# Attention into a mixture of experts: the product with V in plain float32 on 64 columns a head, a third buffer for raw weights, later places for attention's matmuls, last outputs in halves

## The chip, the core and the metric

The kernel runs on one core of a Trainium2 chip. TensorE (PE) does matmuls into PSUM, VectorE (DVE) and ScalarE (ACT) work on SBUF and PSUM, GpSimd (POOL) does two reductions over partitions, and SyncE (SP) issues nearly all transfers. The metric is the time of one execution in microseconds of device time, and lower is better.

## What is computed

Block-causal attention over 4 batches of 8 heads (576 positions, 64 numbers a head), whose output, with the heads side by side, is the input of 4 expert networks; each token mixes the experts by its own probabilities.

```
scores = scale * np.matmul(q, k.transpose(0, 1, 3, 2))
mask = block_i >= block_j              # blocks of 64 positions
scores = np.where(mask, scores, -1000000000.0)
attn = np.exp(scores - max); attn = attn / (sum + 1e-09)
x = np.matmul(attn, v)                 # -> [2304, 512]
...
for e in range(4):
    h = np.maximum(x @ w1[e], 0.0)     # 512 -> 1024
    out += p[:, e:e + 1] * (h @ w2[e]) # 1024 -> 512
```

(Condensed; all in float32.)

## The kernel before

**Tokens.** The 2304 tokens are worked on in five blocks: block 0 holds the first 64 positions of all batches (256 tokens), blocks 1 to 4 hold positions 64 to 575 of one batch each (512 tokens). For a block, the experts run as 32 chunks (4 experts by 8 slices of 128 hidden units). A chunk is 12 matmuls x·w1 into a bank `h` (`mm1`, line 1035) and, one chunk later, h·w2 into the accumulators `acc` (`mm2`, line 1080: 12 matmuls in blocks 1 to 4, 6 in block 0).

**Split numbers.** The experts' operands are split into a high and a low part, and three products (high·high, high·low, low·high) in a fast float32 form ("fp32r") stand for one float32 product. For the weights, ACT or DVE casts the raw tile to its high part (line 340), and DVE subtracts to get the low part (line 347: `w1l`, `w2l`). Raw tiles lie in `w1r` and `w2r`, two buffers each; a buffer is free again when its low part is done. After mm1, ACT makes `hh` (line 1052) and DVE `hl` (line 1054).

**Attention** runs beside the experts, one block ahead, in 16 units (4 head pairs of 4 batches). Units 0 to 3 run beside block 0 and are "plain"; units 4 to 15 run beside blocks 1 to 3 and are "split". In all of them keys lie on the partitions of the score tile `S`, queries along it: five pieces of 512, 448, 320, 192 and 64 columns, for two heads. A unit multiplies Q and K into PSUM banks `att` (lines 527; 539 and 540 in split units), copies each bank to `S` (ACT mostly) and takes the running maximum `cm` on DVE; POOL reduces the maximum over partitions (line 696); DVE subtracts it; ACT takes exponentials. There are two `att` banks, and a split unit fills seven banks' worth of scores, so a bank's next product waits until ACT and DVE have read the bank.

The product with V differs. In plain units, exponentials are taken piece by piece, plain float32 matmuls multiply them with V, head 0 into partitions 0 to 63 of a bank and head 1 into 64 to 127 (line 777, 64 columns of V each), and another four matmuls with ones sum the probabilities. In split units, each head's probabilities are split into `PH` and `PL` and V into `VS`; per head, four matmuls with PH, one with the last 64 keys in plain float32 and four with PL (line 809) make a bank whose upper and lower halves are added. The sums come from POOL (line 733), after the pieces have been added up in `S`.

**Order.** All engines' instruction lists come from one planner (`Flow`) that simulates engines with estimated costs and picks the next instruction. `late(op, by)` adds `by` ns to the distance that it wants from the instructions that an operation depends on, and half of it to the distance from the last use of the operation's buffers (`est`, line 107). Score products of split units have `LAG` = 1500, the products with V of split units half of it, plain units none. Engines run their lists strictly in order.

Of the kernel before, what the change touches and what calls it, by code (L numbers as in the profile page):

```python
# [15 lines left out]
MASK_BLOCK = 64  # L16
# [20 lines left out]
LAG = 1500.0  # L37
# [34 lines left out]
class Flow:  # L72
# [134 lines left out]
def kernel(  # L207
# [65 lines left out]
    bufs("w1r", 2, [P, KC, P])  # L273
    bufs("w2r", 2, [P, DM])
# [7 lines left out]
    bufs("vr", 1, [P, MAXT, 2, D])  # L282
# [5 lines left out]
    bufs("VS", 2, [P, MAXT, 4, D], F32R)  # L288
    bufs("VJ", 2, [P, 2, 3, D])
# [94 lines left out]
    def unit(u, ua, us, ju, pu, ph, job, dst, c):  # L384
# [5 lines left out]
        wide, narrow = [x for x in pcs if x[2] > NARROW and not plain], [x for x in pcs if x[2] <= NARROW or plain]  # L390
        ce = sum(x[2] for x in wide)
# [67 lines left out]
        def v_thread():  # L459
            yield ("until", lambda: now[0] >= gate[u])  # L460
            vals, jv, got = [], [], []
            n = len(wide)
            VS = None
            VJ = yield (fl.take("VN", u) if plain else fl.take("VJ", us))
            if n:
                vr = yield fl.take("vr", us)
                VS = yield fl.take("VS", us)
                for h in range(2):
                    vals.append((yield dma(vr.tile[:, :n, h, :], v[b, h0 + h, :P * n].rearrange("(t p) d -> p t d", p=P),
                                           n * P * 256, u=[vr], prio=pr + 0.005)))  # L470
            keep = sorted(j for j, *_ in narrow if j is not None)
            for h in range(2):
                if plain:
                    jv.append((yield dma(VJ.tile[:, VJ.tile.shape[1] - 1, 2 * h, :], v[b, h0 + h, q1 - P:q1], P * 256,
                                         u=[VJ], prio=pr + 0.005)))
                elif odd:
                    jv.append((yield dma(VJ.tile[64 * h:64 * h + 64, VJ.tile.shape[1] - 1, 1, :], v[b, h0 + h, q1 - MASK_BLOCK:q1], 64 * 256,
                                         u=[VJ], prio=pr + 0.005)))
                if keep:
                    jv.append((yield dma(VJ.tile[:, :len(keep), 2 * h, :],  # L480
                                         v[b, h0 + h, P * keep[0]:P * keep[-1] + P].rearrange("(t p) d -> p t d", p=P),
                                         len(keep) * P * 256, u=[VJ], prio=pr + 0.005)))
            if n:
                vs = VS.tile[:, :n]
                a = yield a_copy(vs[:, :, 0:4:3, :], vr.tile[:, :n], n * 128, vals, [vr, VS], pr + 0.005)
                l = yield tt(BOTH, vs[:, :, 1:3, :], vr.tile[:, :n], vs[:, :, 0:4:3, :], SUB, n * 128, [a], [vr, VS],
                             pr + 0.005)
                got += [a, l]
                fl.give(vr)
            st["v"] = (VS, VJ, got, jv)  # L490

# [18 lines left out]
        def s_thread():  # L510
# [31 lines left out]
            for h, ps_list in banks:  # L542
                if plain:
# [15 lines left out]
                    m = yield op("pe", 300.0 + (2 * sum(ws) + ws[0] - sum(abs(x - y) for x, y in zip(ws, ws[1:]))) / 1.2,  # L559
                                 fn, need(0), [*two, KK] + Q, pr)  # L560
# [94 lines left out]
        def by_piece(Sb, Sv, mx, mv, m):  # L655
# [8 lines left out]
            def sum_up():  # L664
# [3 lines left out]
                for i, (_, a, w, c0) in enumerate(todo[1:]):  # L668
# [18 lines left out]
        def m_thread():  # L687
# [13 lines left out]
            st["P"] = {}  # L701
            st["exp"] = []

            if plain:
                yield from by_piece(Sb, Sv, mx, mv, m)
                return
            subs = []
            for _, a, w, c0 in pcs:
                sv, mb = Sv[:, :, c0:c0 + w], mv[:, :, a - q0:W]
                subs.append((yield tt("dve", sv, sv, mb, SUB, 2 * w, [m] + st["evac"], [Sb, mx], pr)))  # L710
            fl.give(mx)

            def exp_head(h):
                PH = PL = a = l = None
                j = yield op("act", 0.833 * C + 95, lambda _: nc.scalar.activation(
                    Sv[:, h, :C], Sv[:, h, :C], AF.Exp, scale=scale), subs, [Sb], pr)
                if wide:
                    PH = yield fl.take("PH", pu + h)
                    PL = yield fl.take("PL", pu + h)
                    a = yield a_copy(PH.tile[:, :ce], Sv[:, h, :ce], ce, [j], [Sb, PH], pr)  # L720
                    l = yield tt("dve", PL.tile[:, :ce], Sv[:, h, :ce], PH.tile[:, :ce], SUB, ce, [j, a], [Sb, PH, PL], pr)
                st["P"][h] = (PH, PL, a, l, Sb, j)

            for h in range(2):
                yield from exp_head(h)

            got = [x for h in range(2) for x in st["P"][h][2:4] + st["P"][h][5:]]
            for _, a, w, c0 in pcs[1:]:
                acc = Sv[:, :, a - q0:W]
                got = [(yield tt("dve", acc, acc, Sv[:, :, c0:c0 + w], ADD, 2 * w, got, [Sb], pr))]  # L730
            st["sums"] = []
            for h in range(2):
                st["sums"].append((yield op("pool", 150 + 6.3 * W, lambda _, h=h: nc.gpsimd.partition_all_reduce(  # L733
                    Sv[:, h, W:2 * W], Sv[:, h, :W], P, RED.add), got, [Sb], pr)))
# [3 lines left out]
        fl.spawn(pv_flow(st, q0, dst, c, W, wide, narrow, C, plain, pr, bank_tag))  # L738
# [13 lines left out]

    def pv_flow(st, q0, dst, c, W, wide, narrow, C, plain, pr, bank_tag):
        yield ("until", lambda: "v" in st)
        VS, VJ, vv, jv = st["v"]
        xs = yield fl.take("xs")
        rc = yield fl.take("rc", st["ua"])
        parts, sums = [], []
        if plain:
            yield ("until", lambda: "sums" in st)  # L760
            sa, sv = st["sums"]
            PJ, pj = st["P"][1][4:]
            two = []
            for _ in range(2):
                two.append((yield fl.take("att", None, bank_tag)))

            def fn(_):

                for x, todo in zip(two, (narrow, [(None, None, W, 0)])):
                    for i, (j, _a, w, c0) in enumerate(todo):  # L770
                        for g in range(2):
                            if x is two[0]:
                                lhsT = VJ.tile[:, VJ.tile.shape[1] - 1 if j is None else j, 2 * g, :]
                                rhs = PJ.tile[:, g * C + c0:g * C + c0 + w]
                            else:
                                lhsT, rhs = VJ.tile[:, 0, 1, :], sa.tile[:, g * W:g * W + W]
                            nc.tensor.matmul(out=x.tile[64 * g:64 * g + 64, W - w:W], lhsT=lhsT, rhs=rhs,  # L777
                                             start=(i == 0), stop=(i == len(todo) - 1))

            m = yield op("pe", 450.0 + (C + W) / 0.6, fn, jv + pj + sv, [*two, VJ, PJ, sa], pr)  # L780
# [8 lines left out]
            sums.append((yield op([("act", 0.833 * W + 55), ("dve", 1.04 * W + 70)], 0, fn, [m], [two[1], rc], pr)))  # L789
            parts.append((yield a_copy(xs.tile[:, :W], two[0].tile[:, :W], W, [m], [two[0], xs], pr, True)))  # L790
            fl.give(*two)
        for h in range(0 if plain else 2):
            yield ("until", lambda: h in st.get("P", ()))
            PH, PL, a, l, PJ, pj = st["P"][h]
            pb = yield fl.take("att", None, bank_tag)
            ps = pb.tile
# [416 lines left out]
```

## Time and profile before

| | |
|---|---|
| median of 3 runs | 931.5 us (931.19 to 933.13) |
| the profiled execution | 932.45 us, of which its span is 930.7 us |
| granted TensorE clock, mean | 0.999 of full speed |
| HBM read / written | 102.40 MB / 4.72 MB |

The span runs from the first to the last instruction of the profile; the 1.75 us between it and the execution's time lie around it. Busy time of an engine is time with at least one instruction on it; a matmul's duration in the profile includes the pipeline's depth, so the pace of matmuls is read from one start to the next.

### The profile page before, as it was taken

How to read it: one execution, taken by the hardware profiler on the slowest of the kernel's cores; microseconds unless marked ns; L12 is line 12 of the kernel's file. 1: busy time of each engine (PE TensorE's matmuls, PEld its weight loads, DVE VectorE, ACT ScalarE, POOL GpSimd, SP SyncE). 2: the span in 40 equal slices, each digit the busy share in tenths (PEclk: the TensorE clock that was granted, in tenths of full speed). 3: DMA queues.
4: the chain of work that ended last, by engine and by line, in shares of the span. 5: the costliest groups of instructions: out<-in, count | busy, mean ns of one | idle time of the engine just before them, and what ended most of it. 6: DMA issues, size and time to landing. Idle time of an engine off the chain costs nothing.

```text
span 930.7 us, 12721 instructions
## 1 busy us (share of the span) xinstructions
PE 915.3 (98%) x4398; PEld 750.8 (81%) x4398; DVE 728.9 (78%) x1291; ACT 438.2 (47%) x774; POOL 138.7 (15%) x57
## 2 busy tenths in 40 slices
PE   8999999999999999999999999999999999999998
PEld 4677788888887888887888888888888888888886
DVE  7789999989897888878988888888988754445442
ACT  3577765655463454454454545464534322322220
POOL 1111101222103201212131202012121200000000
PEclk9999999999999999999999999999999999999999
DMA  9755466534532445351623545343423343333321
GB/s 166 181 163 165 136 154 189 116 115 93 145 85 80 113 140 137 108 135 46 149 72 100 128 121 154 104 105 113 116 90 90 92 148 102 92 100 94 100 57 45
DMA packets 236162, 107.97 MB, mean 116 GB/s; under 512 B 131393, under 2 KB 213313, under 8 KB 236097
## 3 DMA queue, kind: packets, MB, share of 16 engines
q1 hardware_dynamic: 232928, 106.38, 42.8%
q10 hardware_dynamic: 3168, 0.79, 0.5%
q8 instruction: 34, 0.56, 0.2%
q14 instruction: 32, 0.25, 0.1%
HBM read 102.40 MB, written 4.72 MB: 115 GB/s over the span
## 4 chain that ended last, share of the span: by engine, by line
PE 90%; DVE 4%; DMA 3%; ACT 1%; issue 1%; SPq 1%; DVEq 0%; ACTq 0%
PE acc L1080 40%; PE h L1035 40%; PE att L809 4%; PE att L539 2%; PE att L540 2%; DMA w1r<-in_moe_w_dram 1%; SPq L334 1%; PE acc L777 1%; PE att L777 1%; DVE w2l L347 1%; DMA S<-in_v_dram 1%; DVE cm L347 1%; PE att L527 1%; DVE w1l L347 0%; DMA w2r<-in_moe_w_dram 0%
## 5 line engine op out<-in xcount | busy, mean ns | idle before, releaser
L1035 PE MATMUL h<-xh,w1h 128*128 128x512 f32 (+1 forms) x640 | 237.9, 372 | 0.0
L1035 PE MATMUL h<-xh,w1l 128*128 128x512 f32 (+1 forms) x640 | 236.1, 369 | 1.6 <-DVE w1l L347 1.6
L1035 PE MATMUL h<-xl,w1h 128*128 128x512 f32 (+1 forms) x640 | 235.6, 368 | 0.1
L1080 PE MATMUL acc<-w2h,hh 128*128 128x512 f32 x576 | 227.0, 394 | 0.0
L1080 PE MATMUL acc<-w2h,hl 128*128 128x512 f32 x576 | 224.7, 390 | 1.0 <-DVE hl L1054 1.0
L1080 PE MATMUL acc<-w2l,hh 128*128 128x512 f32 x576 | 224.6, 390 | 0.0
L1052 ACT ACTIVATE hh<-h 128x512 fp32r<-128x512 f32 (+1 forms) x160 | 88.9, 556 | 184.6 <-PE h L1035 183.5
L347 DVE TENSOR_TENSOR w2l<-w2r,w2h 128x512 fp32r<-128x512 f32 x160 | 112.9, 706 | 56.2 <-ACT w2h L340 55.8
L340 ACT CAST w2h<-w2r 128x512 fp32r<-128x512 f32 x148 | 92.2, 623 | 136.1 <-PE acc L1080 132.0
L1035 PEld LDWEIGHTS h<-xh,w1l 128*128 128x128 f32 x640 | 120.4, 188 | 22.7 <-DVE w1l L347 2.4
L1035 PEld LDWEIGHTS h<-xh,w1h 128*128 128x128 f32 x640 | 120.5, 188 | 21.0 <-issue 1.2
L1035 PEld LDWEIGHTS h<-xl,w1h 128*128 128x128 f32 x640 | 120.6, 188 | 19.8 <-DVE xl L347 0.3
L1054 DVE SCALAR_TENSOR_TENSOR hl<-h,hh 128x512 fp32r<-128x512 f32 (+1 forms) x160 | 100.6, 629 | 35.9 <-ACT hh L1052 35.4
L1080 PEld LDWEIGHTS acc<-w2h,hl 128*128 128x128 f32 x576 | 108.1, 188 | 25.0 <-DVE hl L1054 1.9
L1080 PEld LDWEIGHTS acc<-w2h,hh 128*128 128x128 f32 x576 | 108.3, 188 | 23.9 <-issue 2.5
L347 DVE TENSOR_TENSOR w1l<-w1r,w1h 128x512 fp32r<-128x512 f32 x160 | 119.3, 745 | 8.2 <-ACT w1h L340 4.4
L1080 PEld LDWEIGHTS acc<-w2l,hh 128*128 128x128 f32 x576 | 108.3, 188 | 20.0
L733 POOL PARTITION_ALL_REDUCE S<-S x24 | 79.8, 3374 | 242.4 <-DVE S L347 223.9
L696 POOL PARTITION_ALL_REDUCE mx<-cm x16 | 54.4, 3398 | 355.8 <-DVE cm L347 270.3
L340 ACT COPY S<-att 128x512 f32<-128x512 f32 (+2 forms) x90 | 48.7, 542 | 71.3 <-DVE att L609 48.6
L340 ACT CAST w1h<-w1r 128x512 fp32r<-128x512 f32 x116 | 71.6, 619 | 19.4 <-DMA w1r<-in_moe_w_dram 19.1
L347 DVE TENSOR_TENSOR S<-S,mx 128x1024 f32<-128x1024 f32 (+4 forms) x80 | 60.0, 790 | 5.4 <-POOL mx L696 5.4
(135 smaller groups left out, 862.3 us busy)
## 6 DMA issues: line engine op xcount, KB each, us to landing
w1r<-in_moe_w_dram SPq DMA_DIRECT2D x160, 256.0 KB, 2.8
w2r<-in_moe_w_dram SPq DMA_DIRECT2D x160, 256.0 KB, 2.8
qr<-in_q_dram SPq DMA_DIRECT2D x112, 64.0 KB, 2.3
kr<-in_k_dram SPq DMA_DIRECT2D x64, 72.0 KB, 2.8
out_dram<-o SPq DMA_DIRECT2D x16, 256.0 KB, 2.3
vr<-in_v_dram SPq DMA_DIRECT2D x24, 128.0 KB, 2.6
VN<-in_v_dram SPq DMA_DIRECT2D x8, 128.0 KB, 3.1
S<-in_k_dram SPq DMA_DIRECT2D x4, 128.0 KB, 4.7
```

The lines of the kernel that those rows point to most:

```text
L340: o = op(engs, 0, lambda e: nc.scalar.copy(dst, src) if e == "act" else nc.vector.tensor_copy(dst, src), r, u, prio)
L347: o = op(engs, 0, lambda e: ENG[e].tensor_tensor(out=dst, in0=a, in1=b, op=alu), r, u, prio)
L539: nc.tensor.matmul(out=o, lhsT=KK.tile[:, at:at + n], rhs=Hv[:, hs, lo:W], start=True, stop=False)
L540: nc.tensor.matmul(out=o, lhsT=KK.tile[:, at:at + n], rhs=Lv[:, hs, lo:W], start=False, stop=True)
L696: lambda _: nc.gpsimd.partition_all_reduce(mx.tile[:, :2 * W], src, P, RED.max),
L733: st["sums"].append((yield op("pool", 150 + 6.3 * W, lambda _, h=h: nc.gpsimd.partition_all_reduce(Sv[:, h, W:2 * W], Sv[:, h, :W], P, RED ...
L777: nc.tensor.matmul(out=x.tile[64 * g:64 * g + 64, W - w:W], lhsT=lhsT, rhs=rhs, start=(i == 0), stop=(i == len(todo) - 1))
L809: nc.tensor.matmul(out=o, lhsT=lhsT, rhs=rhs, start=(i == 0), stop=(i == n - 1))
L1035: nc.tensor.matmul(out=ps[:, :n], lhsT=s.tile[:, ks], rhs=x.tile[:, kc, :n], start=(kc == 0 and m == 0), stop=(kc == KC - 1 and m == 2),)
L1052: a = yield op("act", 0.833 * n + 55, lambda _: nc.scalar.activation(hh.tile[:, :n], ps[:, :n], AF.Relu), [mm], [pb, hh], 0.0)
L1054: l = yield op("dve", 1.04 * n + 70, lambda _: nc.vector.scalar_tensor_tensor(out=hl.tile[:, :n], in0=ps[:, :n], scalar=0.0, in1=hh.tile[: ...
L1080: nc.tensor.matmul(out=acc, lhsT=s.tile[:, ts], rhs=w.tile, start=(f == 0 and m == 0), stop=(f == FC - 1 and m == 2))
```

## The change

- Split units now do the product with V as plain units do: float32 matmuls, 64 columns a head, both heads in one bank, probabilities straight from `S`. PH, PL, VS, VJ and the additions of halves are gone. The sums of split units stay with POOL, but are taken from `sa`, the tile in which plain units add up their pieces, into a new tile `sb`. Exponentials are taken piece by piece in all units.
- `w1r` and `w2r` get a third buffer.
- `LAG` becomes 2000, the planner wants the whole lag (not half) from a buffer's last use, and plain units' score products get half a LAG.
- In the last block, the last expert's multiply-and-add of each token tile and its transfer to memory are done in two halves of 256 columns, on the queues of SP and ACT.

```diff
-LAG = 1500.0
+LAG = 2000.0
...
-                if b.base + self.LAT + op.lag / 2 > t:
-                    t = b.base + self.LAT + op.lag / 2
+                if b.base + self.LAT + op.lag > t:
+                    t = b.base + self.LAT + op.lag
...
-    bufs("w1r", 2, [P, KC, P])
-    bufs("w2r", 2, [P, DM])
+    bufs("w1r", 3, [P, KC, P])
+    bufs("w2r", 3, [P, DM])
...
+    bufs("sb", 1, [P, 2 * MAXW])
...
+                sb = yield fl.take("sb", us)
+                sums = []
                 for h in range(2):
-                    st["P"][h] = (None, None, None, None, Sb, exps)
-                st["sums"] = (sa, got)
+                    sums.append((yield op("pool", 150 + 6.3 * W, lambda _, h=h: nc.gpsimd.partition_all_reduce(
+                        sb.tile[:, h * W:h * W + W], sa.tile[:, h * W:h * W + W], P, RED.add), got, [sa, sb], pr)))
+                fl.give(sa)
+                st["sums"] = (sb, sums)
...
-                    m = yield op("pe", 300.0 + (2 * sum(ws) + ws[0] - sum(abs(x - y) for x, y in zip(ws, ws[1:]))) / 1.2,
-                                 fn, need(0), [*two, KK] + Q, pr)
+                    m = yield late(op("pe", 300.0 + (2 * sum(ws) + ws[0] - sum(abs(x - y) for x, y in zip(ws, ws[1:]))) / 1.2,
+                                 fn, need(0), [*two, KK] + Q, pr), LAG / 2)
...
+            for x, todo in zip(two, (pcs, [(None, None, W, 0)])):
+                for i, (j, _a, w, c0) in enumerate(todo):
+                    for g in range(2):
+                        if x is two[0]:
+                            lhsT = VJ.tile[:, j, 2 * g, :] if j is not None else VJ.tile[:, nj, 2 * g if plain else 1, :]
+                            rhs = PJ.tile[:, g * C + c0:g * C + c0 + w]
+                        else:
+                            lhsT, rhs = VJ.tile[:, 0, 1, :], sa.tile[:, g * W:g * W + W]
+                        nc.tensor.matmul(out=x.tile[64 * g:64 * g + 64, W - w:W], lhsT=lhsT, rhs=rhs,
+                                         start=(i == 0), stop=(i == len(todo) - 1))
+
+        m = yield late(op("pe", 450.0 + (C + (W if plain else 0)) / 0.6, fn, jv + pj + sv,
+                          [*two, VJ, PJ] + ([sa] if plain else []), pr), 0.0 if plain else LAG / 2)
...
-            for x, split, dep in ((PH, True, a), (PJ, False, pj), (PL, True, l)):
...
-            x = yield a_copy(rc.tile[hi, :W], ps[lo, :W], W, [m], [pb, rc], pr, True)
-            parts.append((yield tt("dve", xs.tile[hi, :W], ps[hi, :W], rc.tile[hi, :W], ADD, W, [m, x], [pb, rc, xs], pr)))
...
+        if e == E - 1 and bi == len(BLOCKS) - 1:
+
+            (p0, tok, n), = segments(bi, t)
+            o = outs[bi, t]
+            for x, q_ in enumerate(("sp", "act")):
+                c = slice(DM // 2 * x, DM // 2 * (x + 1))
+                d = yield op("dve", 1.04 * DM / 2 + 130, lambda _, c=c: nc.vector.scalar_tensor_tensor(
+                    out=o.tile[:, c], in0=acc[:, c], scalar=pn, in1=o.tile[:, c], op0=MUL, op1=ADD), [mm], [o], 0.0)
+                yield dma(out[tok:tok + n, c], o.tile[p0:p0 + n, c], n * DM * 2, [d], [o], 6.0, q_)
+            return
```

On PE, at a split unit's product with V (unit 7), the order before is two groups a head with expert matmuls (lines 1035 and 1080) around them; this is head 0:

```order
L1035 MATMUL h_123<-xh_90,w1l_66 128x512
L809 MATMUL att_128<-PH_115,VS_104 128x512
L809 MATMUL att_128<-PH_115,VS_104 128x448
L809 MATMUL att_128<-PH_115,VS_104 128x320
L809 MATMUL att_128<-PH_115,VS_104 128x192
L809 MATMUL att_128<-S_112,VJ_106 128x64
...
L809 MATMUL att_128<-PL_113,VS_104 128x512
L809 MATMUL att_128<-PL_113,VS_104 128x448
L809 MATMUL att_128<-PL_113,VS_104 128x320
L809 MATMUL att_128<-PL_113,VS_104 128x192
L1080 MATMUL acc_126<-w2h_69,hh_81 128x512
```

On PE, a unit's whole product with V in the change is one run of ten matmuls, of which each row stands for both heads:

```order
L718 MATMUL att_123<-S_109,VN_105 64x512 x2
L718 MATMUL att_123<-S_109,VN_105 64x448 x2
L718 MATMUL att_123<-S_109,VN_105 64x320 x2
L718 MATMUL att_123<-S_109,VN_105 64x192 x2
L718 MATMUL att_123<-S_109,VN_105 64x64 x2
```

Eighteen matmuls a unit have become ten, each with 64 columns of V instead of 128.

On PE, at the score products of unit 7's second head before, the bank `att_129` is used for the pieces of 320 and 192, then 15 expert matmuls and the two of the other bank stand ahead of its next use, the piece of 448:

```order
L540 MATMUL att_129<-LL_102,KK_100 128x192
...
L1035 MATMUL h_123<-xh_90,w1l_66 128x512
L539 MATMUL att_128<-HH_101,KK_100 128x512
L540 MATMUL att_128<-LL_102,KK_100 128x512
...
L1035 MATMUL h_123<-xl_92,w1h_62 128x512
L1035 MATMUL h_123<-xh_90,w1l_66 128x512
L539 MATMUL att_129<-HH_101,KK_100 128x448
```

At the same place of the change (where the roles of the two banks are swapped) 21 expert matmuls stand between them:

```order
L507 MATMUL att_122<-LL_103,KK_101 128x192
...
L506 MATMUL att_123<-HH_102,KK_101 128x512
L507 MATMUL att_123<-LL_103,KK_101 128x512
...
L998 MATMUL acc_119<-w2h_70,hl_86 128x512
L506 MATMUL att_122<-HH_102,KK_101 128x448
```

So a bank's next product has moved back by six expert matmuls here.

On SP's queue, early in the program, before (`w1r_78` and `w2r_80` are chunk 1's weights, `w1r_77` and `w2r_79` chunk 2's, `kr_94` keys and `VN_108` values of the next unit):

```order
L334 DMA w1r_78<-in_moe_w_dram 128x4x128
L334 DMA w2r_80<-in_moe_w_dram 128x512
L334 DMA kr_94<-in_k_dram 32x18x32 x3
L334 DMA w1r_77<-in_moe_w_dram 128x4x128
L334 DMA kr_94<-in_k_dram 32x18x32
L334 DMA VN_108<-in_v_dram 128x64
L334 DMA w2r_79<-in_moe_w_dram 128x512
```

and in the change, where chunk 2 has buffers of its own (`w1r_79`, `w2r_82`) and `w1r_77` and `w2r_80` already hold chunk 3's:

```order
L324 DMA w1r_78<-in_moe_w_dram 128x4x128
L324 DMA w1r_79<-in_moe_w_dram 128x4x128
L324 DMA w2r_81<-in_moe_w_dram 128x512
L324 DMA w2r_82<-in_moe_w_dram 128x512
L324 DMA kr_96<-in_k_dram 32x18x32
L324 DMA w1r_77<-in_moe_w_dram 128x4x128
L324 DMA kr_96<-in_k_dram 32x18x32 x2
```

Chunk 2's weights have moved ahead of the next unit's keys, and chunk 3's among them.

## Rows read from the trace of the kernel before

**Rows 1.** The page: span, and each engine's busy time with instruction count.

```profile
span 930.7 us, 12721 instructions
PE 915.3 (98%) x4398; PEld 750.8 (81%) x4398; DVE 728.9 (78%) x1291; ACT 438.2 (47%) x774; POOL 138.7 (15%) x57
```

**Rows 2.** Windows: stretch, length, engines' busy time (instructions), granted clock, DMA share, GB/s.

```profile
22.60:150.00 127.40, 123.64 (x763) 96.48 (x762) 114.20 (x218) 90.20 (x202) 13.42 (x4) 1.00 0.61 162
150.00:750.00 600.00, 597.14 (x2746) 498.13 (x2745) 515.96 (x888) 300.08 (x487) 120.76 (x36) 1.00 0.42 112
```

**Rows 3.** Waits of PE: waiting line <- what ended it: us in total, times, longest.

```profile
PE att L539 <- DVE cm L347: 2.8, 4, 1.1
...
PE h L1035 <- DVE w1l L347: 1.6, 3, 0.8
PE acc L1080 <- DVE hl L1054: 1.0, 1, 1.0
...
PE att L527 <- ACT cm L340: 0.7, 1, 0.7
```

**Rows 4.** The chain of waits, at 754.75 us: start, us, what.

```profile
754.75 2.72 PE h L1035 x12
```

**Rows 5.** Timeline of PE at a split unit's product with V, head 0: start, us, instruction.

```profile
172.28 0.84 PE L809 MATMUL att<-PH,VS 128*128 128x512 f32 x4
...
173.44 0.39 PE L1035 MATMUL h<-xl,w1h 128*128 128x512 f32 x1
...
174.59 0.83 PE L809 MATMUL att<-PL,VS 128*128 128x512 f32 x4
...
175.51 0.39 PE L1080 MATMUL acc<-w2l,hh 128*128 128x512 f32 x1
```

**Rows 6.** Timeline of PE at a plain unit's product with V and sums.

```profile
82.94 0.39 PE L1080 MATMUL acc<-w2h,hl 128*128 128x512 f32 x1
83.26 2.81 PE L777 MATMUL att<-S,VN 128*64 128x512 f32 x20
85.90 1.03 PE L777 MATMUL acc<-sa,VN 128*64 128x512 f32 x4
86.86 0.38 PE L1035 MATMUL h<-xh,w1h 128*128 128x256 f32 x1
87.08 0.28 PE L1035 MATMUL h<-xl,w1h 128*128 128x256 f32 x1
```

**Rows 7.** Groups by form: instruction, count, busy us, mean ns, idle time before.

```profile
L809 PE MATMUL att<-PL,VS 128*128 128x512 f32 x24 | 10.4, 432 | 0.0
...
L347 DVE TENSOR_TENSOR PL<-S,PH 128x1472 fp32r<-128x1472 f32 x24 | 40.3, 1682 | 0.2
...
L340 ACT CAST PH<-S 128x1472 fp32r<-128x1472 f32 x13 | 18.6, 1430 | 0.3
```

**Rows 8.** Timeline of PE at its longest wait for a bank.

```profile
284.18 0.39 PE L1035 MATMUL h<-xh,w1l 128*128 128x512 f32 x1
285.62 0.44 PE L539 MATMUL att<-HH,KK 128*128 128x448 f32 x1 [1.06 <-DVE cm L347]
```

**Rows 9.** Timeline of DVE just before that wait ends.

```profile
281.10 2.85 DVE L347 TENSOR_TENSOR w2l<-w2r,w2h 128x512 fp32r<-128x512 f32 x1
283.87 0.69 DVE L830 STREAM_TRANSPOSE tr<-S 64x512 f32<-64x512 f32 x1
284.60 0.88 DVE L347 TENSOR_TENSOR cm<-att,cm 128x320 f32<-128x320 f32 x2
```

**Rows 10.** Timeline of POOL at the same time, and the group of w2l's on DVE.

```profile
277.64 6.75 POOL L733 PARTITION_ALL_REDUCE S<-S  x2 [23.21 <-DVE S L347]
...
L347 DVE TENSOR_TENSOR w2l<-w2r,w2h 128x512 fp32r<-128x512 f32 x160 | 112.9, 706 | 56.2 <-ACT w2h L340 55.8
```

**Rows 11.** Groups of the page: ACT's casts of w1, their idle time before and its releaser.

```profile
L340 ACT CAST w1h<-w1r 128x512 fp32r<-128x512 f32 x116 | 71.6, 619 | 19.4 <-DMA w1r<-in_moe_w_dram 19.1
```

**Rows 12.** The program's end: DVE's timeline, a group of half-size operations, output transfers (page).

```profile
924.11 2.79 DVE L1116 SCALAR_TENSOR_TENSOR o<-acc,probs_n,o 128x512 f32<-128x512 f32 x4 [2.08 <-PE acc L1080]
...
L1054 DVE SCALAR_TENSOR_TENSOR hl<-h,hh 128x256 fp32r<-128x256 f32 x32 | 13.2, 412 | 1.1 <-ACT hh L1052 0.9
...
out_dram<-o SPq DMA_DIRECT2D x16, 256.0 KB, 2.3
```

More of the change, by code (lines that the diff above doesn't have):

```diff
@@ L460, in v_thread @@
             yield ("until", lambda: now[0] >= gate[u])
[L461 to L470, printed above, removed]
@@ L471, in v_thread @@
-            keep = sorted(j for j, *_ in narrow if j is not None)
-            for h in range(2):
[L473 to L490, printed above, removed]
+            jv = []
+            VJ = yield fl.take("VN", u)
+            at = VJ.tile.shape[1] - 1
@@ L492, in unit @@
+            for h in range(2):
+                r, o, n = (slice(0, P), 2 * h, P) if plain else (slice(64 * h, 64 * h + 64), 1, MASK_BLOCK)
+                jv.append((yield dma(VJ.tile[r, at, o, :], v[b, h0 + h, q1 - n:q1], n * 256, u=[VJ], prio=pr + 0.005)))
+                jv.append((yield dma(VJ.tile[:, :nt, 2 * h, :], v[b, h0 + h, :P * nt].rearrange("(t p) d -> p t d", p=P),
+                                     nt * P * 256, u=[VJ], prio=pr + 0.005)))
+            st["v"] = (VJ, jv)
         banks = []
@@ L700, in m_thread @@
             mv = mx.tile[:, :2 * W].rearrange("p (h w) -> p h w", h=2)
[L701 to L734, printed above, removed]
+            yield from by_piece(Sb, Sv, mx, mv, m)
         for t in (k_thread, q_thread, v_thread, s_thread, e_thread, m_thread):
             fl.spawn(t())
-        fl.spawn(pv_flow(st, q0, dst, c, W, wide, narrow, C, plain, pr, bank_tag))
+        fl.spawn(pv_flow(st, q0, dst, c, W, pcs, C, plain, pr, bank_tag))
     def x_take(bi):
@@ L748, in x_take, with pv_flow @@
         yield ("until", lambda: X[bi] is not None)
-    def pv_flow(st, q0, dst, c, W, wide, narrow, C, plain, pr, bank_tag):
+    def pv_flow(st, q0, dst, c, W, pcs, C, plain, pr, bank_tag):
         yield ("until", lambda: "v" in st)
-        VS, VJ, vv, jv = st["v"]
+        VJ, jv = st["v"]
+        nj = VJ.tile.shape[1] - 1
         xs = yield fl.take("xs")
         rc = yield fl.take("rc", st["ua"])
-        parts, sums = [], []
-        if plain:
[L760 to L780, printed above, removed]
@@ new lines, in pv_flow, with fn @@
+        yield ("until", lambda: ("sums" if plain else "P") in st)
+        PJ, pj = st["P"]
+        sa, sv = st["sums"] if plain else (None, [])
+        two = []
+        for _ in range(2 if plain else 1):
+            two.append((yield fl.take("att", None, bank_tag)))
+        def fn(_):
+            for x, todo in zip(two, (pcs, [(None, None, W, 0)])):
[8 more added lines that the diff above has]
+                                         start=(i == 0), stop=(i == len(todo) - 1))
@@ L781, in pv_flow @@
+        m = yield late(op("pe", 450.0 + (C + (W if plain else 0)) / 0.6, fn, jv + pj + sv,
+                          [*two, VJ, PJ] + ([sa] if plain else []), pr), 0.0 if plain else LAG / 2)
+        fl.give(VJ, PJ)
+        if plain:
             fl.give(sa)
@@ L787, in fn @@
                     nc.vector.tensor_scalar_add(rc.tile[:, :W], ps[:, :W], 1e-9)
[L789 to L796, printed above, removed]
-            todo = []
-            for x, split, dep in ((PH, True, a), (PJ, False, pj), (PL, True, l)):
-                for j, _a, w, c0 in wide if split else narrow:
-                    if split:
-                        lhsT, cost, dv, c1 = VS.tile[:, j, 2 * h:2 * h + 2, :], w / 2.4 + PEO, vv, c0
-                    else:
-                        nj = VJ.tile.shape[1] - 1
-                        lhsT = VJ.tile[:, nj, 1 - h:3 - h, :]
-                        cost, dv, c1 = 2 * max(107.0, 2 * w / 2.4 + 2.5), jv, h * C + c0
-                    todo.append((lhsT, x.tile[:, c1:c1 + w], w, cost, dv + [dep]))
-            for i, (lhsT, rhs, w, cost, dep) in enumerate(todo):
-                def fn(_, o=ps[:, W - w:W], lhsT=lhsT.rearrange("p g d -> p (g d)"), rhs=rhs, i=i, n=len(todo)):
-                    nc.tensor.matmul(out=o, lhsT=lhsT, rhs=rhs, start=(i == 0), stop=(i == n - 1))
-                m = yield late(op("pe", max(107.0, cost), fn, dep, [pb] + [x for x in (VS, VJ, PH, PL, PJ) if x], pr), LAG / 2)
-            hi, lo = slice(64 * h, 64 * h + 64), slice(64 - 64 * h, 128 - 64 * h)
-            fl.give(PH, PL)
-            x = yield a_copy(rc.tile[hi, :W], ps[lo, :W], W, [m], [pb, rc], pr, True)
-            parts.append((yield tt("dve", xs.tile[hi, :W], ps[hi, :W], rc.tile[hi, :W], ADD, W, [m, x], [pb, rc, xs], pr)))
-            fl.give(pb)
-        fl.give(VJ, PJ) if plain else fl.give(VS, VJ)
+            sums = yield op([("act", 0.833 * W + 55), ("dve", 1.04 * W + 70)], 0, fn, [m], [two[1], rc], pr)
+        part = yield a_copy(xs.tile[:, :W], two[0].tile[:, :W], W, [m], [two[0], xs], pr, True)
+        fl.give(*two)
         rt, n = rc.tile, W // 32
@@ L824, in pv_flow @@
         if plain:
-            got = yield op("dve", 1.04 * W + 70, lambda _: nc.vector.transpose(out=t1, in_=rt[:, :W]), sums, [rc, tr], pr)
+            got = yield op("dve", 1.04 * W + 70, lambda _: nc.vector.transpose(out=t1, in_=rt[:, :W]), [sums], [rc, tr], pr)
         else:
-            yield ("until", lambda: len(st.get("sums", ())) == 2)
-            for h, s in enumerate(st["sums"]):
+            yield ("until", lambda: "sums" in st)
+            sb, sums = st["sums"]
+            for h, s in enumerate(sums):
                 hi = slice(64 * h, 64 * h + 64)
                 got = yield op("dve", 1.04 * W + 70, lambda _, h=h, hi=hi: nc.vector.transpose(
-                    out=t1[hi], in_=PJ.tile[hi, h * C + W:h * C + 2 * W]), [s], [PJ, tr], pr)
-            fl.give(PJ)
+                    out=t1[hi], in_=sb.tile[hi, h * W:h * W + W]), [s], [sb, tr], pr)
+            fl.give(sb)
             got = yield op("dve", 80.0, lambda _: nc.vector.tensor_scalar_add(t2, t0, 1e-9), [got], [tr, tc_], pr)
@@ L838, in pv_flow @@
         fl.give(tr, tc_)
-        d = yield tt("dve", xs.tile[:, :W], xs.tile[:, :W], rt[:, :W], MUL, W, parts + got, [xs, rc], pr)
+        d = yield tt("dve", xs.tile[:, :W], xs.tile[:, :W], rt[:, :W], MUL, W, [part] + got, [xs, rc], pr)
         fl.give(rc)
@@ L1175 @@
                 nc.gpsimd.memset(t[64 * h:64 * h + 64, :, 64 - 64 * h:128 - 64 * h], 0.0)
-        for tag in ("VN", "VJ"):
-            for b in fl.free[tag]:
-                if tag == "VN":
-                    nc.gpsimd.memset(b.tile[:, :, 1, :], 1.0)
-                    continue
-                n = b.tile.shape[1] - 1
-                nc.gpsimd.memset(b.tile[:, :n, 1, :], 0.0)
-                nc.gpsimd.memset(b.tile[:, n, 0:3:2, :], 0.0)
+        for b in fl.free["VN"]:
+            nc.gpsimd.memset(b.tile[:, :, 1, :], 1.0)
         fl.run()
```

15 lines of the change are left out of this document (4 added, 11 removed).

## Prediction

> **What bounds the kernel now.** I read the page first: TensorE is busy 915.3 of 930.7 us, DVE 728.9, ACT 438.2 [rows 1]. TensorE is the bound, so a part of the change counts only if it shortens TensorE's own work, removes a wait of TensorE, or moves the last transfer. The windows show that DVE is close behind beside block 0 (114.20 of 127.40 us) and has room beside blocks 1 to 3 (515.96 of 600.00) [rows 2]. Then the waits of TensorE [rows 3]. Those that the change can touch are the split units' score products for their banks (2.8 us in 4), weights' low parts (1.6 in 3), one `hl` (1.0) and one plain unit's score product (0.7): 6.1 us in 9 waits. The list names no product with V. A wait costs more than its listed idle time, since the listed time leaves out the pipeline's end: in [rows 8] the two starts are 1.44 us apart where the pace would be 0.23, so 1.21 is lost where 1.06 is listed. With 0.15 more for each of the nine, the four groups cost 3.4, 2.05, 1.15 and 0.85 us, 7.45 in all. The pace of a 512-column matmul is 2.72 us / 12 = 0.227 us [rows 4].
>
> **1. The product with V.** Before, head 0 takes, from the first PH product to the second expert matmul behind it, 173.44 - 172.28 = 1.16 us, of which one expert matmul is 0.227: 0.93. The PL group takes 175.51 - 174.59 = 0.92, less 0.227: 0.69. That is 1.62 us a head [rows 5]. There are 24 heads (the count of the PL group [rows 7]), so 38.9 us.
>
> The change's form stands in this trace, in the plain units: the same five widths, float32, 64 columns a head, two heads in one bank [rows 6]. Its 20 hardware matmuls take 85.90 - 83.26 = 2.64 us. Entering costs 83.26 - 82.94 - 0.227 = 0.09; leaving, the expert matmul behind takes 0.22 us where a 256-column one takes about half of 0.227: 0.10. The sums' four matmuls need 0.96 us for 512 columns a head, where a third of 2.64 would be 0.88, so the pipeline's end adds 0.08. Together 2.91 us a unit, 34.9 in 12 units. TensorE saves 38.9 - 34.9 = **4.0 us**. A reading of a start is good to 0.01 or 0.02 us, and it enters some five times; I keep 3.0 and 4.6 as bounds.
>
> **2. Banks of the split units' scores.** The longest wait shows how these come about. The bank's reader on DVE, `cm`, ran from 284.60, because a `w2l` at 281.10 took 2.85 us and a transpose 0.69 [rows 9]; `w2l` takes 0.706 us in the mean, and POOL's two sums ran from 277.64 to 284.39 [rows 10]. So DVE was held some 2.1 us beside POOL, and TensorE came for the bank after 15 expert matmuls. In the change 21 stand there, 6 x 0.227 = 1.36 us more than the wait of 1.21. In front of DVE, the low parts of PH go as well (24 x 1.68 = 40.3 us), so its queue is shorter. POOL's 24 sums stay, and will hold DVE elsewhere. Of 3.4 us I take **2.6** back and leave one wait of 0.8; bounds 0 and 3.4.
>
> The Trainium skill ("SBUF — State Buffer", section "SBUF: two separate sides") says that a DVE operation with two inputs in SBUF and a GpSimd operation that reads SBUF exclude each other, and that the later one is blocked until the other ends. The trace agrees that such an operation is held (2.85 us for `w2l`). By that rule one could be held for a whole reduction, 6.75 / 2 = 3.4 us, more than the new room, and part 2 would give nothing (925.1 us in all); by the row it is held for 2.1.
>
> **3. Third raw buffers, and later products of plain units.** Beside block 0, ACT stood 19.1 us waiting for w1 to land over the whole run [rows 11], and TensorE waited for low parts. With three buffers, chunk 2's weights are issued ahead of the next unit's keys and chunk 3's among them, and every split can run about a chunk earlier: 2.7 us in block 0, for 12 half-width matmuls and 6 whole ones at 0.227. That covers the longest of these waits, 0.8. I take 1.7 of 2.05 us back. The plain score product's wait of 0.7 us meets a lag of 1.0 us more: 0.5 of 0.85. The `hl` that TensorE waited for stands behind as long a queue on DVE as before (more weight splits have moved ahead of it): nothing. Together **2.2 us**; bounds -2 (the splits in front delay `hl` by three more operations of 0.7) and 4.05.
>
> **4. The end.** DVE's last four operations end at 926.90, 0.70 apart [rows 12]. As two halves the last tile takes at most 2 x 0.412 = 0.82 us [rows 12], so the last half comes up to 0.1 us later, and its transfer is half as large; a whole one lands 2.3 us after issue [rows 12], of which I can't tell how much is size. I take **0.2 us** gained, nearer to the row of the whole tile than to half of it; bounds -0.1 and 1.0.
>
> **5. What costs nothing.** Five exponentials in place of two a unit, and `sa`'s copy, are ACT's, which is busy 47%, and lose PH's casts (13 x 1.43 us on ACT alone [rows 7]). If ACT's room were gone, they would delay the product with V, which stands at least 60 expert matmuls (13.6 us) behind the unit's last score product in both orders. `sb` lets POOL read and write other tiles in the same 24 calls: nothing.
>
> **Sum.** 4.0 + 2.6 + 2.2 + 0.2 = 9.0 us. The profiled execution took 932.45, so 923.45; the median shown is 0.95 lower, so the forecast is **922.5 us**.
>
> **Rivals.**
> *A. The waits move and stay.* POOL's reductions hold DVE at other places, and other banks and low parts are late: parts 2 and 3 give nothing. For it: no reduction is removed, and the 2.1 us that DVE lost is more than the 1.36 us of new room. Against it: DVE loses 40 us of work. Part 1 and 4 alone: 931.5 - 4.2 = 927.3.
> *B. Slower: early splits block DVE.* Engines run in order. In the change, weight splits stand further ahead in DVE's and ACT's lists, and if their transfers land no earlier, since all share one bandwidth of 162 GB/s in this stretch [rows 2], `hl` waits behind them and TensorE for `hl`. The place is chunks 2 to 8. The most that rows allow is that all 19.1 us in which ACT waited for w1 pass on to TensorE: 931.5 - 4.0 - 2.6 - 0.2 + 19.1 = 943.8. It decides the sign when more than 6.8 us pass on. Against it: before, hardly any did.
> *C. The float32 products don't overlap in split units.* If the two heads ran one behind the other, a unit would take 2 x 2.64 + 0.27 = 5.55 us, 2.3 more than now, 27.6 in 12 units: 931.5 + 27.6 - 5.0 = 954.1. Against it stands [rows 6], where both heads' 1536 columns are through in 2.64 us, in the same widths. The Trainium skill ("FP8 and Floating Point Precision", section "TensorE Precision Notes") gives true float32 four passes through the array; by that rule, without the overlap, this case would hold. The trace agrees with four passes only if both heads share them: 1536 x 4 / 2.4 GHz is 2.56 us, beside 2.64 measured.
> *D. More.* All nine waits go: 4.0 + 7.45 + 0.2 = 11.65, 919.9; with part 1's and 4's upper bounds 918.5.
>
> **Chances.** The forecast (920.5 to 926): 0.66. A: 0.16. D: 0.09. B: 0.06, two thirds of it slower. C: 0.02. 0.01 is left. The range of 8 in 10 takes in the forecast, A and most of D: 919 to 928. About 0.2% (1.9 us) is what a measurement of this kernel can tell from no change: faster means below 929.6. That holds for the forecast, D and nearly all of A: 0.90; same 0.05; slower 0.05.
>
> **What would show it.** In the changed profile a split unit's product with V should read 20 matmuls in 2.64 us on TensorE, with the expert matmuls around it 0.09 and 0.1 late; otherwise part 1 is wrong. The waits of TensorE should name score products for at most one or two banks with about 0.8 us in all, and `w1l` for under 0.4; three or more waits of a microsecond speak for A. `hl` or `w1l` waits above 3 us between 25 and 60 us speak for B. DVE should lose at least 40 us of busy time beside blocks 1 to 3. The last transfer should be issued within 0.2 us of the old distance to TensorE's last matmul. The prediction is wrong if the plain form costs more between fp32r neighbours with two `att` banks than in block 0, or if new waits for exponentials appear ahead of the product with V.

## Result, and the profile after

The changed kernel takes 921.62 us in the median of 4 runs (920.5 to 922.4), the kernel before 932.26 in the same comparison: a ratio of 0.9886, 95% interval 0.9868 to 0.9903, or 9.0 to 12.3 us. The profiled execution took 922.09 (span 920.3). The forecast was 922.5, range 919 to 928.

The page, as in [rows 1]:

```profile
span 920.3 us, 12670 instructions
PE 910.2 (99%) x4398; PEld 731.8 (80%) x4398; DVE 659.7 (72%) x1235; ACT 409.0 (44%) x774; POOL 139.4 (15%) x53
```

DVE lost 69 us. The windows of [rows 2]:

```profile
22.60:150.00 127.40, 125.35 (x775) 99.08 (x774) 114.78 (x219) 90.77 (x200) 13.18 (x4) 0.99 0.65 170
150.00:750.00 600.00, 600.00 (x2785) 485.21 (x2784) 454.95 (x840) 272.62 (x494) 122.16 (x36) 1.00 0.43 114
```

Beside blocks 1 to 3 DVE lost 61.0 us of work (515.96 to 454.95) and TensorE is without a gap. Beside block 0 DVE is as full as before. The waits of PE, whole list:

```profile
PE att L813 <- DMA S<-in_k_dram: 2.1, 1, 2.1
PE h L953 <- DVE xl L337: 1.5, 1, 1.5
PE att L862 <- DVE o L858: 0.8, 2, 0.5
PE h L349 <- PEq L1121: 0.8, 1, 0.8
PE acc L875 <- ACT xs L330: 0.5, 1, 0.5
```

Of the nine waits that the change could touch [rows 3] none is left. One is new: the first expert matmuls wait 1.5 us for `xl`. A split unit's product with V, in PE's timeline (start, us, instruction):

```profile
180.55 0.39 PE L953 MATMUL h<-xh,w1l 128*128 128x512 f32 x1
180.87 2.81 PE L718 MATMUL att<-S,VN 128*64 128x512 f32 x20
183.61 0.50 PE L953 MATMUL h<-xh,w1h 128*128 128x512 f32 x1
183.95 0.39 PE L953 MATMUL h<-xl,w1h 128*128 128x512 f32 x1
```

From 180.55 to 183.95 are 3.40 us, less two expert matmuls at 0.227: 2.95 us a unit, where 2.91 was forecast. The start, in PE's and then DVE's timeline:

```profile
24.22 0.36 PE L953 MATMUL h<-xh,w1h 128*128 128x256 f32 x1
...
25.01 0.28 PE L953 MATMUL h<-xh,w1h 128*128 128x256 f32 x1
26.82 0.38 PE L953 MATMUL h<-xl,w1h 128*128 128x256 f32 x1 [1.53 <-DVE xl L337]
...
28.47 0.41 PE L953 MATMUL h<-xl,w1h 128*128 128x256 f32 x1
28.68 0.41 PE L953 MATMUL h<-xh,w1l 128*128 128x256 f32 x1
```

```profile
24.22 0.43 DVE L330 CAST w1h<-w1r 128x512 fp32r<-128x512 f32 x1 [0.68 <-DMA w1r<-in_moe_w_dram]
24.68 0.69 DVE L337 TENSOR_TENSOR w1l<-w1r,w1h 128x512 fp32r<-128x512 f32 x1
25.29 0.42 DVE L330 CAST w2h<-w2r 128x512 fp32r<-128x512 f32 x1
25.74 0.69 DVE L337 TENSOR_TENSOR w2l<-w2r,w2h 128x512 fp32r<-128x512 f32 x1
26.35 0.42 DVE L337 TENSOR_TENSOR xl<-acc,xh 128x256 fp32r<-128x256 f32 x1
```

The last `xl` of block 0 stands behind two weight splits; the first of them, chunk 2's w1, is there because of the third raw buffer, and waited 0.68 us for its transfer besides. Half a microsecond after the wait the matmuls of 256 columns run 0.21 us apart, 0.12 before it. The windows of this stretch (the last three figures are granted clock, DMA share and GB/s):

```profile
24.00:26.00 2.00, 1.29 (x11) 1.08 (x10) 1.71 (x4) 0.73 (x2) 0.00 (x0) 1.00 0.50 98
26.00:28.00 2.00, 1.18 (x7) 1.18 (x8) 2.00 (x5) 0.41 (x2) 0.00 (x0) 0.85 0.93 217
28.00:30.00 2.00, 2.00 (x12) 2.00 (x10) 1.55 (x4) 0.74 (x2) 0.00 (x0) 0.50 0.59 125
30.00:32.00 2.00, 2.00 (x10) 1.09 (x11) 1.09 (x2) 1.19 (x3) 0.00 (x0) 0.80 0.09 9
```

The clock fell to 0.50, its lower level of 1.2 GHz, and cost, at 2 us a window times the share of the clock that is missing, 0.3 + 1.0 + 0.4 = 1.7 us. With the wait, the start lost 3.2 us.

ACT's casts of w1, as in [rows 11]:

```profile
L330 ACT CAST w1h<-w1r 128x512 fp32r<-128x512 f32 x100 | 61.2, 615 | 1.9 <-DMA w1r<-in_moe_w_dram 1.3
```

The wait for w1 fell from 19.1 to 1.3 us. At the end, from the last matmul's start (915.53) to the end of the span are 4.77 us, 4.98 before (925.72 to 930.7).

### The profile page after: what moved, and what is told of

It is laid out like the page before. It is cut to its first block, busy times and chain, and to the rows that moved or that the text cites. A ratio compares the mean times of both kernels' runs of the same rounds, so it can differ in the third digit from the quotient of the medians.

```text
span 920.3 us, 12670 instructions
## 1 busy us (share of the span) xinstructions
PE 910.2 (99%) x4398; PEld 731.8 (80%) x4398; DVE 659.7 (72%) x1235; ACT 409.0 (44%) x774; POOL 139.4 (15%) x53
## 4 chain that ended last, share of the span: by engine, by line
PE 96%; DMA 2%; SPq 1%; DVE 0%; issue 0%; DVEq 0%; ACT 0%
PE h L953 43%; PE acc L998 43%; PE att L718 4%; PE att L507 2%; PE att L506 2%; PE att L494 1%; PE acc L718 1%; SPq L324 1%; DMA w1r<-in_moe_w_dram 1%; DMA S<-in_v_dram 1%; PE acc L494 0%; DMA cm<-in_q_dram 0%; DVE o L1027 0%; PE att L556 0%; DVE w1l L337 0%
## 5 line engine op out<-in xcount | busy, mean ns | idle before, releaser
L337 DVE TENSOR_TENSOR w1l<-w1r,w1h 128x512 fp32r<-128x512 f32 x160 | 108.8, 680 | 4.7
L651 POOL PARTITION_ALL_REDUCE sb<-sa x24 | 82.2, 3472 | 146.5 <-DVE sa L337 117.0
L330 ACT CAST w1h<-w1r 128x512 fp32r<-128x512 f32 x100 | 61.2, 615 | 1.9 <-DMA w1r<-in_moe_w_dram 1.3
```

The costliest lines, as they stand in the source:

```text
L330: o = op(engs, 0, lambda e: nc.scalar.copy(dst, src) if e == "act" else nc.vector.tensor_copy(dst, src), r, u, prio)
L337: o = op(engs, 0, lambda e: ENG[e].tensor_tensor(out=dst, in0=a, in1=b, op=alu), r, u, prio)
L651: sums.append((yield op("pool", 150 + 6.3 * W, lambda _, h=h: nc.gpsimd.partition_all_reduce(sb.tile[:, h * W:h * W + W], sa.tile[:, h * W ...
```

## Experiments

Each was timed beside the kernel before. "Ratio" is to that kernel, with its 95% interval.

| run | median us | ratio |
|---|---|---|
| the change | 921.62 | 0.9886 [0.9868, 0.9903] |
| pv_only | 925.62 | 0.9920 [0.9908, 0.9933] |
| lag_only | 928.71 | 0.9961 [0.9948, 0.9974] |
| oldlag | 922.43 | 0.9886 [0.9873, 0.9900] |
| raw2 | 927.02 | 0.9934 [0.9920, 0.9947] |
| whole_end | 920.05 | 0.9868 [0.9852, 0.9884] |
| heads_apart | 947.57 | 1.0163 [1.0147, 1.0178] |
| pv_twice | 952.13 | 1.0207 [1.0193, 1.0222] |
| hold2 | 921.49 | 0.9882 [0.9868, 0.9895] |
| hold2_oldlag | 925.30 | 0.9927 [0.9911, 0.9942] |
| hold2_lag25 | 920.85 | 0.9870 [0.9854, 0.9885] |
| raw4 | 920.05 | 0.9866 [0.9850, 0.9883] |
| hold2_raw4 | 920.76 | 0.9864 [0.9849, 0.9878] |

### The product's price: heads_apart and pv_twice

heads_apart, in split units alone (its list is then walked by head):

```diff
-                for i, (j, _a, w, c0) in enumerate(todo):
-                    for g in range(2):
+                order = [(i, g) for i in range(len(todo)) for g in range(2)]
+                if not plain:
+                    order.sort(key=lambda y: y[1])
+                for i, g in order:
```

> The changed kernel in which a split unit's product with V issues all five matmuls of head 0 and then all five of head 1, instead of the heads in turn; the same matmuls otherwise. Theory: the two heads' matmuls run at the same time, on 64 columns each, only when they are neighbours in the queue; apart, a unit takes about 2 x 2.6 us and the kernel 921.6 + 12 x 2.5 = 951. Rival: what counts is the columns alone, in any order, and the time stays at 921.6.

pv_twice:

```diff
-            for x, todo in zip(two, (pcs, [(None, None, W, 0)])):
+            for x, todo in zip(two if plain else two * 2, (pcs, pcs if not plain else [(None, None, W, 0)])):
```

> The changed kernel in which a split unit's product with V is issued twice in a row (the second time it starts again from nothing, so the output is the same); all else alike. Theory: its 20 matmuls take 2.64 us of TensorE's time, read from the plain units, and nothing else is delayed by them: 12 x 2.64 = 31.7 us more, 921.6 + 31.7 = 953.3. Rival, rival C in part: between split products they cost more than beside block 0, 3 us or more each: 957.6 or more.

heads_apart lost 25.8 us against the change (0.0277 of 932), 2.15 a unit; pv_twice 29.9 us (0.0321), 2.5 a unit. PE's timelines, heads_apart first:

```profile
180.48 5.01 PE L721 MATMUL att<-S,VN 128*64 128x512 f32 x20
185.42 0.50 PE L956 MATMUL h<-xh,w1h 128*128 128x512 f32 x1
```

```profile
180.54 5.40 PE L718 MATMUL att<-S,VN 128*64 128x512 f32 x40
185.87 0.50 PE L953 MATMUL h<-xh,w1h 128*128 128x512 f32 x1
```

The same twenty matmuls take 4.94 us apart and 2.74 in turn, and forty take 5.33, 2.59 more. So the plain form gains only because the heads stand in turn, and between fp32r neighbours it costs what it cost beside block 0. The rival of pv_twice (3 us or more) falls. heads_apart came out 3 us below its expected time: rows give 2.20 a unit, not 2.5.

### The banks: pv_only and lag_only

pv_only is the change with these lines as before, and with the rest of the placing as before too (half a lag behind a bank, none for plain units' score products) and the last outputs whole; lag_only is the kernel before with the whole placing of the change:

```diff
-LAG = 2000.0
+LAG = 1500.0
...
-    bufs("w1r", 3, [P, KC, P])
-    bufs("w2r", 3, [P, DM])
+    bufs("w1r", 2, [P, KC, P])
+    bufs("w2r", 2, [P, DM])
```

> The changed kernel with the third raw buffers, the later placing and the halved last outputs undone, so that only the plain product with V is left. Theory: the product alone gives 3.6 us (12 units at 2.94 us in place of 38.9), so 932.3 - 3.6 = 928.7, and score products still wait for banks, 2 us or more in all, since these waits need the later placing. Rival: what DVE no longer does (the low parts of PH, 40 us) already frees the banks; then no such wait is left and the time is 925.3 (3.4 us lower).

> The kernel before with the later placing alone (2.0 us, whole behind a bank, and the plain units' score products too); its product with V stays split, its raw buffers two. Theory, after the plain product alone had freed every bank: the placing is worth nothing by itself while w1 lands late, since with two raw buffers it cost about 1.3 us (927.0 against 925.6 in the first comparison). It takes away most of the waits for banks (3.4) and brings waits for w1h: 931 to 932, within 0.2% of the kernel before. Rival, the prediction's part 2 in its first half: the six expert matmuls of new room are enough, 933.0 - 2.6 = 930.4 or less, with no new wait.

Waits of PE in pv_only, and then in lag_only:

```profile
PE h L953 <- DVE w1l L337: 2.0, 4, 0.8
...
PE h L953 <- ACT w1h L330: 0.9, 1, 0.9
PE att L494 <- ACT cm L330: 0.9, 1, 0.9
...
PE acc L998 <- DVE hl L972: 0.4, 1, 0.4
```

```profile
PE h L1035 <- DVE w1l L347: 2.2, 5, 0.8
PE h L1035 <- ACT w1h L340: 1.9, 3, 1.0
```

In neither does a split unit's score product wait. pv_only gained 7.5 us (0.0080 of 933), where 3.6 was expected: its theory was wrong and its rival right, the plain product alone frees all the banks. It did so without more room: between a unit's runs of score products stand 3 to 12 expert matmuls, 3 to 21 before. The rival names DVE's relief; but a unit's product with V also takes a bank once now and not twice, and no run separates the two. lag_only gained 3.6 us (0.0039 of 932), as its rival said and more than my theory: the placing alone frees the banks too, though with new waits for w1h, which the rival left out. Either is enough; their gains don't add.

### The third raw buffers and the placing: raw2 and oldlag

raw2 has the second half of the diff above on the change, oldlag its first half (with half a lag behind a bank, and none for plain units).

> The changed kernel with two raw buffers for w1 and for w2 as before. Theory: the waits for w1l come back (2 us), but TensorE's wait of 1.5 us for the last xl of block 0 goes, with the stretch at half speed behind it (1.5 us or more): 921.6 + 2.0 - 3.0 = 920.6. Rival: the third buffers are worth what the prediction gave them and the start is as before in any case: 921.6 + 1.7 = 923.3.

> The changed kernel with only the placing undone (1.5 us as before, and half of it behind a bank). Theory: the waits for banks come back, 2 to 3.4 us, and the plain units' 0.85: 921.6 + 3.5 = 925.1. Rival: DVE's shorter queue is what removed them; then 921.6 within 0.5, and no split score product waits.

Waits of PE in raw2:

```profile
PE h L953 <- ACT w1h L330: 2.9, 2, 2.1
...
PE h L953 <- DVE w1l L337: 1.6, 5, 0.7
```

raw2 lost 4.5 us (0.0048) where I expected a gain of 1. The `xl` wait does go, but w1 is late in block 0: w1l in five waits and w1h in two. With three buffers none of these is left; so they are worth more than their harm at the start. oldlag reads the change's ratio; its list has the same wait of 1.5 us for `xl` and one bank that is 0.2 late. Beside the plain product and the third buffers the placing is worth nothing that this measurement can tell. The theory (3.5 us worse) falls.

### The end: whole_end

```diff
-        if e == E - 1 and bi == len(BLOCKS) - 1:
+        if False:
```

> The changed kernel with the last block's last outputs whole, as before. Theory, from the trace after (4.77 us from the last matmul's start to the end of the span, 4.98 before): 0.2 us slower, which this measurement can hardly tell. Rival: the halves are worth the 1.0 us that was the prediction's upper bound, or cost the 0.1 of its lower.

Its interval overlaps the change's, and the traces don't bear out the 0.2 us either: from the last matmul's start to the end of the span are 4.39 us in whole_end (914.31 to 918.7) and 4.76 in pv_only, both with whole outputs, and 4.55 to 5.11 in the runs with halves. No gain from the halves is shown. The run told something else. Up to its end it issues what the change issues, and yet its first expert matmul starts at 22.36, the change's at 24.22. PE's timeline of whole_end, then of the change, and then of hold2 (below), with the window around it (third figure from the end: granted clock):

```profile
7.37 0.60 PE L813 MATMUL acc<-ident,cm 128*128 128x128 f32 x4
...
22.36 0.36 PE L953 MATMUL h<-xh,w1h 128*128 128x256 f32 x1
```

```profile
8.28 1.06 PE L813 MATMUL acc<-ident,cm 128*128 128x128 f32 x4
```

```profile
8.74 1.06 PE L813 MATMUL acc<-ident,cm 128*128 128x128 f32 x4
8.00:9.00 1.00, 1.00 (x5) 0.53 (x4) 0.69 (x2) 0.16 (x1) 0.00 (x0) 1.00 1.36 192
```

The same four transposes took 0.60 and 1.06 us: the change's profiled execution began at a slower pace, and its granted clock reads 0.50 from 7 to 10 us, 1.00 in whole_end. But hold2 has the slow transposes too, and its first expert matmul at 24.36, under a clock that reads 1.00; pv_only and hold2_lag25 are like it. So the reading of the clock doesn't settle the cause of the slow pace, which stays open. Single executions of one order differ by 1.9 us, and 22.64 in the trace before against 24.22 is no effect of the change.

### The start: hold2, hold2_oldlag, hold2_lag25, raw4, hold2_raw4

hold2 is the change with two lines; hold2_oldlag has the old placing as well, hold2_lag25 LAG = 2500. raw4 has four raw buffers each, hold2_raw4 both.

```diff
         def w_split(which, i, raw, src, v0, pr):
+        if i >= 2:
+            yield ("until", lambda: left_first[0] == 0)
         hi = yield fl.take(f"w{which}h", i)
```

> The changed kernel in which the splits of chunk 2 and later stand behind block 0's attention in program order; nothing else differs, and their loads are issued as before. Theory: the last xl runs ahead of them, TensorE does not wait for it and the granted clock stays up between 24 and 32 us: 921.6 - 3.0 = 918.6. Rival: chunk 2's low part is late instead, or the clock falls in this stretch whatever TensorE waits for: 921 to 922.

> The kernel with chunk 2's splits behind block 0's attention and the placing of before (1.5 us); the plain product, third raw buffers and halved outputs stay. Theory: the start keeps its clock, and as the placing is worth nothing beside the plain product the one hh wait of 1.5 us behind ACT's casts, which came with the last kernel's order, is chance and goes: 921.6 - 2.0 = 919.6. Rival: each new order brings a wait of its own about as long: 921 to 922.

> Three raw buffers, the splits of chunk 2 and later behind block 0's attention, and attention's products placed 2.5 us behind their buffers in place of 2.0. Theory: the one hh wait of 1.5 us in the kernel with 2.0 was due to a crowded list of ACT at one place; another placing spreads it: 919.5 to 920.5. Rival: the wait comes back there or elsewhere: 921 to 922.

> The changed kernel with four raw buffers each. In DVE's list the casts and low parts of w1 for chunks 2 and 3 now both stand ahead of block 0's last xl. Theory (weights split ahead of that xl are what costs the start): TensorE waits for xl longer than 1.5 us, by one cast and one low part and whatever their transfer is late, 2.6 us or more, with a stretch at the lower granted clock behind it: 921.6 + 1.5 to 3 = 923 to 925. Rival: more room for weights helps as the third buffers did: 920 or less.

> Four raw buffers, and the splits of chunk 2 and later behind block 0's attention. The last xl now follows the one before it at once on DVE. Theory: TensorE has no wait for xl, its clock stays up between 24 and 32 us, and with more weights loaded ahead no w1h, w2h or hh is late in block 0: 918 to 919. Rival: as with three buffers and the splits behind, another wait of 1 to 2 us comes up in block 0: 921 to 922.

In hold2 the wait for `xl` shrank to 0.7 us and the clock read 1.00 from 24 to 32 us, as the theory has it; but the time stayed, as its rival has it. The 1.5 us came back at 52 us, where `hh` stands behind casts and exponentials on ACT:

```profile
PE acc L1000 <- ACT hh L972: 1.5, 1, 1.5
```

In hold2_lag25 that wait is gone, as its theory has it, and only 0.5 us for `xl` and 0.2 for a plain unit's bank took its place; its median, 920.85, lies between theory and rival.

hold2_oldlag was slower, against theory and rival. ACT's timeline there:

```profile
43.44 0.62 ACT L330 CAST w2h<-w2r 128x512 fp32r<-128x512 f32 x1 [2.36 <-DMA w2r<-in_moe_w_dram]
...
45.53 0.62 ACT L330 CAST w1h<-w1r 128x512 fp32r<-128x512 f32 x1 [0.99 <-DMA w1r<-in_moe_w_dram]
...
47.36 0.19 ACT L330 COPY cm<-att 128x64 f32<-128x64 f32 x1
```

Two casts waited 3.35 us for transfers, the copy that frees a plain unit's bank stood behind them, and TensorE waited 3.0 us for it; then came a stretch at the lower clock, of which these are two windows:

```profile
48.00:50.00 2.00, 2.00 (x8) 1.14 (x6) 2.00 (x3) 2.00 (x5) 0.00 (x0) 0.50 0.82 156
52.00:54.00 2.00, 2.00 (x8) 1.61 (x7) 1.07 (x3) 1.45 (x4) 0.00 (x0) 0.50 0.81 266
```

raw4 waited 1.3 us for `xl`, not the 2.6 I expected, and was not slower: chunk 3's split took the place of the one of w2, so two stood ahead as in the change, and DVE ran through them without a gap. hold2_raw4 has no wait for `xl`, weights or `hh`; of the block's waits one is left,

```profile
PE att L494 <- DVE qT L434: 1.2, 1, 1.2
```

and its profile has the shortest span of all, 916.8 us. But the intervals of 0.9864, 0.9866 and 0.9870 overlap that of the change's 0.9886, so none is shown to beat it.

## Why the prediction was right

**Part 1** (4.0 us): 12 x 2.95 = 35.4, so 38.9 - 35.4 = 3.5 us, inside the bounds. The 20 matmuls read 2.74 us, not 2.64; 0.08 of that is the pipeline's end, which I had priced apart. Entering and leaving cost 180.87 - 180.55 - 0.227 = 0.09 and 183.95 - 183.61 - 0.227 = 0.11, as forecast. The Trainium skill ("TensorEngine Tiling (Array Packing)", section "Key Properties") says that different tiles work in parallel and that a change of tiling drains the engine; the trace agrees, with 2.74 us against 4.94 for the one and 0.09 and 0.11 for the other.

**Part 2** (2.6 of 3.4): all four waits went, 3.4 us, the upper bound. The step that failed was to leave one for the reductions on POOL. Its two grounds, more room by the placing and the plain product's relief, were both right, and each is enough alone (lag_only, pv_only). Operations of DVE are still held; of `w2l` in the change the least, median and greatest duration in ns:

```profile
L337 DVE TENSOR_TENSOR w2l<-w2r,w2h x160: 623/684/1660, 17.8 to 897.6; 128x512 fp32r<-128x512 f32 x160
```

The change's greatest is 1.66 us, 2.85 before. But shorter holds are not what freed the banks: a `w1l` takes 2.73 us in lag_only and 2.63 in hold2_lag25, and in neither does a split unit's score product wait. The Trainium skill's rule of a block until the other ends ("SBUF — State Buffer", section "SBUF: two separate sides") would have let part 2 give nothing; no run here shows a hold as long as a reduction (the longest operation, 2.85 us, is 2.2 over the usual 0.68; reductions take 3.3 to 3.5).

**Part 3** (2.2): by the traces 0.85, from two errors of opposite sign. All of the 4.05 us came back, `hl` (which I gave nothing) among them; and the start lost 3.2, which I had not seen: net 0.85. I looked for the harm of early splits in chunks 2 to 8 (rival B), and it lay in chunk 0, in front of the last `xl`, where the order of DVE before has one split and the change two. That the start's loss could be won back is not shown: in hold2 the wait moved. That the buffers and not the placing take away the waits for weights is: oldlag keeps the gain, raw2 loses it. `hl` and a plain unit's score product wait in pv_only (0.4 and 0.9 us) but neither in raw2 nor in oldlag, so for these two either is enough.

**Part 4** (0.2): not shown. The 0.2 between the two traces is less than the spread among runs with whole outputs (4.39 to 4.98 us). **Part 5**: no wait for exponentials appeared; nothing, as forecast.

**The sum.** 3.5 + 3.4 + 0.85 = 7.75 us, where 10.6 (9.0 to 12.3) was measured. Late starts cost more than I priced. In the trace before, 12 starts of matmuls come 0.23 us or more behind their pace, 8.5 us in all, against my 7.45 for nine; one of them, 0.26 for `xl`, stayed. And the start behind a late one is late too, by some 0.1 us:

```profile
59.15 0.39 PE L1035 MATMUL h<-xh,w1l 128*128 128x256 f32 x1 [0.82 <-DVE w1l L347]
59.37 0.28 PE L1035 MATMUL h<-xh,w1h 128*128 128x256 f32 x1
```

These are 0.22 us apart, where the pace of 256 columns is 0.12. That makes 0.8 and 1.1, some 1.9 us more; the remaining 1 us lies within the interval and stays open. The runs add up another way: pv_only gained 7.5 us (parts 1 and 2 forecast 6.6), the third buffers with the halves beside it 3.2 (oldlag against pv_only, 0.0034; forecast 1.9), the placing on top nothing (the change against oldlag). That the forecast came within 1 us is partly luck: parts 1, 3 and 4 brought less by the traces than forecast, and part 2 and what I had not priced brought more.

**Rivals.** A (waits move and stay) is out: none of the old ones is left. D had the waits right (all nine go) and missed the start. B happened in small and elsewhere. C is out as a forecast, but its mechanism is real: heads_apart is slower than the kernel before by 1.6%. The Trainium skill's four passes for float32 ("FP8 and Floating Point Precision", section "TensorE Precision Notes") hold for each head within 4%: 2 x 1536 x 4 / 2.4 GHz = 5.12 us, an estimate, beside 4.94 with the heads apart and 2.74 where they share the time.

## What to carry to other kernels

Plain float32 matmuls on half the columns beat the split form here only while the two halves stand in turn in the queue; one loop the other way round cost 25.8 us. Two remedies for one wait, more room in the order and a product that asks less of DVE and of the banks, don't add: either alone took all of it. A deeper load buffer moves work forward in the lists of in-order engines; look for what now stands behind it at the start, where the list has no slack, before the places that it was meant for.

## What the hardware showed unexpectedly

Short stalls of TensorE can cost as much again in clock, but don't always. After 1.53 us idle (the change), 1.3 (raw4), 2.1 (raw2) and 3.0 (hold2_oldlag), a stretch at the lower level, 1.2 GHz, followed; after 1.5 us at 52 us in hold2 and 1.2 in hold2_raw4 the windows behind read 1.00, and matmuls of 256 columns stand 0.12 us apart. PE's timeline of raw4, matmuls 0.21 us apart behind the wait:

```profile
24.72 0.58 PE L953 MATMUL h<-xl,w1h 128*128 128x256 f32 x1 [1.32 <-DVE xl L337]
...
25.53 0.41 PE L953 MATMUL h<-xl,w1h 128*128 128x256 f32 x1
25.75 0.41 PE L953 MATMUL h<-xh,w1l 128*128 128x256 f32 x1
```

What decides between the two is open. The other surprise was the 1.9 us between two executions of the same order, most of it from a slower pace of the matmuls up to 10 us. Six of the profiles begin so, and the granted clock shows it in three of them only.
